# Attention followed by a squared-ReLU FFN on one core: the FFN's second and first matmuls issued in groups of two units

## The chip, the cores and the metric

The kernel runs on 1 core of one Trainium2 chip. The metric is the device time of one launch in microseconds (us), as a median over runs. Before the change it is 187.35 us (three runs: 187.19, 187.35 and 187.91 us).

## What is computed

```python
def phi(x):                                   # S1, S2: 8 x 32
    a = einsum('rd,bhsd->bhsr', S1, x); b = einsum('rd,bhsd->bhsr', S2, x)
    return einsum('bhsi,bhsj->bhsij', a, b).reshape(*x.shape[:-1], 64)
q_p, k_p = phi(q), phi(k)                     # batch 4, heads 4, seq 1088, head_dim 32
kv  = einsum('bhsf,bhsd->bhfd', k_p, v); z = sum(k_p, axis=2)
num = einsum('bhsf,bhfd->bhsd', q_p, kv)
den = einsum('bhsf,bhf->bhs', q_p, z)[..., None] + 1e-06
x   = (num / den) as 4352 tokens x 128
out = square(relu(x @ w_in)) @ w_out          # w_in 128 x 2048, w_out 2048 x 128
```

The inputs and the output are float32. Nearly all arithmetic is in the last line: two matmuls of 4352 x 128 x 2048.

## The kernel before

**Tiling of the FFN.** The 4352 tokens are cut into ten chunks of 256, 384, 448, 448, five of 512, and 256 columns (list FC). The 2048 hidden features are 16 blocks of 128. A *unit* is a piece of one chunk that fills at most one PSUM bank of 512 columns: with 384, 448 or 512 tokens a unit is one hidden block (m = 1), with 256 tokens two blocks (m = 2), except that the first two units of the first chunk have one. There are NU = 145 units: 9, then 16 for each of the eight middle chunks, then 8.

**One unit's work.** mm1 (function ffn1, matmul at L589): the first matmul, w_in block times xT, into a PSUM tile pg. Both operands are float32r; it stands in the trace as one MATMUL for each hidden block. relu (L598): ScalarE (ACT) reads pg from PSUM and writes gt in SBUF. square: gt to g2, on ACT (L606) or VectorE (DVE, L608). mm2 (function ffn2, L627; L622 in the last chunk, with the operands swapped): w_o block times g2, added up over the 16 blocks in a PSUM tile po. Its operands are float32, and it stands in the trace as two MATMULs with a weight load each. When a chunk is done, DVE transposes po (L631) and SyncE stores it (L641).

**Buffers.** pg has 2 PSUM buffers, po 2, gt 4 and g2 6. So mm1 of unit u must wait for relu of unit u-2, and relu of unit u for the square of unit u-4.

**Attention.** For each of the four batches DVE, POOL, ACT and TensorE make the next columns of xT while the FFN of earlier columns runs. On TensorE these are short blocks of small float32 matmuls: kc (L344), kvp (L408), qc (L304) and nd (L542).

**What sets the order.** Each operation is entered in a planner (class `_Order`) with an engine, an estimated duration, a priority and its dependencies; `run` plays the schedule through and emits the instructions in the order of the planned starts. Each engine then executes its own list strictly in that order. For the FFN's matmuls the order is not left to the priorities: a list `seq` is written out by hand (L1055 to L1060), and each matmul is bound to start after the one ahead of it (L1061, L1062). LU = 4 is the lead: mm1 of the first four units comes first, and then mm2 of unit u goes with mm1 of unit u+4, one matmul of each in turn. Where m = 1 that gives mm2(u), mm1(u+4), mm2(u+1), mm1(u+5) and so on. The planner puts attention blocks between these and decides for each square whether ACT or DVE takes it.

Of the kernel before, what the change touches and what calls it, by code (L numbers as in the profile page):

```python
# [104 lines left out]
def kernel(  # L105
# [20 lines left out]
    LU = 4  # L126
# [440 lines left out]
    units, first_unit, dur = [], {}, []  # L567
# [11 lines left out]
    NU = len(units)  # L579
# [21 lines left out]
    def square(u, eng):  # L601
        w = units[u][2] * units[u][4]
        g2 = fpool.tile([128, 512], F32, tag="g2", bufs=G2, name="g2")
        gt = st["gt", u]
        if eng == "ACT":
            nc.scalar.activation(g2[:, 0:w], gt[:, 0:w], Square)  # L606
        else:
            nc.vector.tensor_tensor(out=g2[:, 0:w], in0=gt[:, 0:w], in1=gt[:, 0:w], op=mult)  # L608
        g2s[u] = g2
# [392 lines left out]
    pe1, pe2 = [], []  # L1002
    ends = (NU - 2, NU - 1)
    for u in range(NU):
        ci, c0, n, d0, m = units[u]
        w = n * m
# [7 lines left out]
        for i in range(m):  # L1014
# [14 lines left out]
            lambda eng, u=u: square(u, eng), uses=[("relu", u)], rings=[("g2", G2)],  # L1029
# [23 lines left out]
    hm = len(pe2[-1]) // 2  # L1053
    pe2[-2], pe2[-1] = pe2[-2][:hm] + pe2[-1][:hm], pe2[-2][hm:] + pe2[-1][hm:]
    seq = [x for u in range(LU) for x in pe1[u]]  # L1055
    for u in range(NU):
        p, q_ = list(pe2[u]), list(pe1[u + LU]) if u + LU < NU else []
        while p or q_:
            seq += p[:1] + q_[:1]
            p, q_ = p[1:], q_[1:]  # L1060
    for x, y in zip(seq, seq[1:]):  # L1061
        O.by_name[y]["soft"].append(O.by_name[x])  # L1062
    O.run()
# [30 lines left out]
```

## Time and profile before

| | |
|---|---|
| runs | 187.19, 187.35, 187.91 us; median 187.35 us |
| the profiled execution: span from the first to the last instruction | 186.2 us |
| median of the runs less that span | 1.15 us |
| granted TensorE clock over the span | 1.000 |
| TensorE matmul busy | 180.4 us (97%) |
| ACT busy | 147.1 us (79%) |
| DVE busy | 108.6 us (58%) |
| squares on ACT / on DVE | 122 / 23 |
| relus | 145 |

The page does not give the profiled execution's own device time beside its span; what lies around the span is taken as the difference to the median. Matmuls are pipelined, and their recorded spans overlap, so the starts of matmuls that follow each other say more than the durations. A weight load (PEld) starts when the matmul ahead of its own has begun to stream: the weights that it overwrites are then in use no longer. "idle before" in an instruction's row is the time that its engine had nothing to do, with what ended it.

### The profile page before, as it was taken

To read this page: it belongs to the slowest core of one execution; us is meant where nothing else is said; L and a number is where in the kernel's file an instruction comes from. 1 tells how busy PE (TensorE), PEld (TensorE's weight loads), DVE (VectorE), ACT (ScalarE), POOL (GpSimd) and SP (SyncE) were. 2 spreads that over 40 slices of the span, in tenths; PEclk is the share of its full clock that TensorE was granted. 3 is DMA by queue.
4 is the path that set the end of the run, shared out by engine and by line. 5 is a ranking of instruction groups with operands and counts; after the bars stand their busy time and mean duration, and the time that the engine had idled before them with its cause. 6 is when DMAs were issued, how large, how long until landed. Compare 5 with 4: busy or idle time off the path is not lost.

```text
span 186.2 us, 3768 instructions
## 1 busy us (share of the span) xinstructions
PE 180.4 (97%) x1417; PEld 105.2 (56%) x1418; DVE 108.6 (58%) x242; ACT 147.1 (79%) x281; POOL 36.5 (20%) x162
## 2 busy tenths in 40 slices
PE   8998999999999999999999999999999999999991
PEld 2766766656555566454554545554545554555791
DVE  4979979969982599599324972997122113112210
ACT  3518769868978887797899897897999999988960
POOL 2745405328300000860000003820000000000000
PEclk9999999999999999999999999999999999999999
DMA  5799800100049500001871200002103000300211
GB/s 185 192 297 310 192 4 5 28 4 0 0 55 267 130 2 4 4 0 24 200 186 19 42 0 4 0 0 38 22 0 58 0 0 0 56 0 0 32 28 28
DMA packets 24673, 11.25 MB, mean 60 GB/s; under 512 B 18000, under 2 KB 23120, under 8 KB 24656
## 3 DMA queue, kind: packets, MB, share of 16 engines
q1 hardware_dynamic: 24144, 10.82, 25.0%
q10 hardware_dynamic: 512, 0.20, 0.4%
q8 instruction: 11, 0.18, 0.4%
q14 instruction: 6, 0.05, 0.1%
HBM read 8.78 MB, written 2.23 MB: 59 GB/s over the span
## 4 chain that ended last, share of the span: by engine, by line
PE 90%; DMA 4%; SPq 1%; POOL 1%; issue 1%; DVE 0%; ACT 0%; ACTq 0%
PE po L627 60%; PE pg L589 18%; PE nd L542 3%; DMA w_in<-in_moe_w_in_dram 3%; PE kvp L408 2%; PE pol L622 2%; PE po L622 2%; PE qc L304 2%; DMA s_nat<-in_S_dram 2%; PE kc L344 1%; SPq L194 1%; POOL sfk L789 0%; ACT gt L598 0%; POOL w_in L671 0%; SPq L203 0%
## 5 line engine op out<-in xcount | busy, mean ns | idle before, releaser
L627 PE MATMUL po<-g,w_o 128*128 128x512 f32 (+3 forms) x288 | 133.0, 546 | 0.3 <-PE pg L589 0.3
L589 PE MATMUL pg<-xT,w_in 128*128 128x512 f32 (+3 forms) x160 | 104.8, 665 | 0.6 <-ACT gt L598 0.5
L598 ACT ACTIVATE gt<-pg 128x512 f32<-128x512 f32 (+3 forms) x145 | 80.7, 561 | 21.7 <-PE pg L589 21.2
L606 ACT ACTIVATE g<-gt 128x512 f32<-128x512 f32 (+2 forms) x122 | 71.8, 603 | 2.7
L627 PEld LDWEIGHTS po<-g,w_o 128*128 128x128 f32 x288 | 53.0, 189 | 30.0 <-issue 19.8
L589 PEld LDWEIGHTS pg<-xT,w_in 128*128 128x128 f32 x160 | 30.1, 189 | 31.7 <-issue 14.3
L608 DVE TENSOR_TENSOR g<-gt 128x512 f32<-128x512 f32 (+3 forms) x23 | 15.1, 660 | 45.9 <-ACT gt L598 45.9
L449 POOL COPY kv<-kvt 32x64 f32<-32x64 f32 x48 | 11.7, 243 | 65.4 <-DVE kvt L426 63.3
L503 POOL COPY rd<-rc 32x9 f32<-32x9 f32 (+2 forms) x80 | 16.7, 209 | 13.1 <-DVE rc L495 9.8
L512 DVE STREAM_SHUFFLE qa<-qc 128x576 f32<-128x576 f32 (+2 forms) x20 | 11.6, 652 | 0.0
L527 DVE TENSOR_TENSOR qp<-qa,qb 128x576 f32<-128x576 f32 (+2 forms) x20 | 10.8, 603 | 0.0
L475 DVE STREAM_TRANSPOSE qt<-qc 128x576 f32<-128x576 f32 (+2 forms) x10 | 5.8, 615 | 5.8 <-PE qc L304 5.8
L631 DVE STREAM_TRANSPOSE oT<-po 128x512 f32<-128x512 f32 (+3 forms) x9 | 5.9, 655 | 5.0 <-PE po L627 5.0
L361 DVE TENSOR_TENSOR kp<-fs 128x576 f32<-128x576 f32 x12 | 8.4, 752 | 0.1
L542 PE MATMUL nd<-qp,kv 32*32 32x288 f32 (+2 forms) x320 | 6.8, 353 | 0.0
L559 DVE TENSOR_TENSOR xT<-nd,bc 128x576 fp32r<-128x576 f32 (+2 forms) x10 | 5.6, 600 | 0.9 <-PE nd L542 0.7
L512 DVE STREAM_SHUFFLE qb<-qc 128x576 f32<-128x576 f32 (+2 forms) x10 | 6.0, 648 | 0.0
L542 PEld LDWEIGHTS nd<-qp,kv 32*32 32x32 f32 x320 | 3.8, 103 | 3.8 <-issue 2.2
L297 DVE STREAM_TRANSPOSE qT<-qn 128x192 f32<-128x192 f32 (+3 forms) x11 | 5.9, 566 | 0.0
L552 DVE STREAM_TRANSPOSE bc<-rd 128x576 f32<-128x576 f32 (+2 forms) x10 | 5.8, 602 | 0.2
L622 PE MATMUL pol<-w_o,g 128*128 128x128 f32 x32 | 5.7, 275 | 0.0
L622 PE MATMUL po<-w_o,g 128*128 128x128 f32 x32 | 5.7, 274 | 0.0
(96 smaller groups left out, 92.3 us busy)
## 6 DMA issues: line engine op xcount, KB each, us to landing
kn<-in_k_dram SPq DMA_DIRECT2D x3, 544.0 KB, 5.4
qn<-in_q_dram SPq DMA_DIRECT2D x3, 544.0 KB, 6.9
vn<-in_v_dram SPq DMA_DIRECT2D x9, 144.0 KB, 5.5
w_in<-in_moe_w_in_dram SPq DMA_DIRECT2D x4, 256.0 KB, 5.2
w_o<-in_moe_w_out_dram SPq DMA_DIRECT2D x4, 256.0 KB, 7.1
out_dram<-oT SPq DMA_DIRECT2D x12, 64.0 KB, 2.0
out_dram<-oT SPq DMA_DIRECT2D x8, 56.0 KB, 1.9
out_dram<-oT SPq DMA_DIRECT2D x8, 48.0 KB, 1.8
```

The source lines that it names most:

```text
L361: nc.vector.tensor_tensor(out=_ap(st[b, "kp"], 0, 128, 64 * NT * h, [[64, NT], [8, 8], [1, 8]]), in0=_ap(fs, 0, 128, o, [[32, NT], [1, 8], ...
L449: nc.gpsimd.tensor_copy(_ap(st[b, "kv"], 32 * c, 32, 64 * h, [[32, E], [1, 32]]), _ap(st["kvt"], 32 * h, 32, 0, [[64, E], [1, 32]]),)
L503: nc.gpsimd.tensor_copy(st[b, "rd", i0][32 * h : 32 * h + 32, n * c : n * c + n], st["rc"][32 * c : 32 * c + 32, n * h : n * h + n],)
L512: nc.vector.stream_shuffle(in_=banks(st[b, "qc", i0], 2 * x, 0, m), out=_ap(st[b, which, i0], 0, 128, 2 * m * x, [[m, 2], [1, m]]), mask=m ...
L527: nc.vector.tensor_tensor(out=st[b, "qp", i0, e][:, r], in0=st[b, f"qa{e}", i0][:, r], in1=st[b, "qb", i0][:, r], op=mult,)
L542: nc.tensor.matmul(nd[32 * h : 32 * h + 32, 512 * c : 512 * c + m], kv[r, o : o + 32], qp[r, m * h : m * h + m], start=(e == 0), stop=(e = ...
L589: nc.tensor.matmul(st["pg", u][:, n * i : n * i + n], w_in[:, 128 * (d0 + i) : 128 * (d0 + i) + 128], xT[:, c0 : c0 + n],)
L598: nc.scalar.activation(gt[:, 0:w], st["pg", u][:, 0:w], Relu)
L606: nc.scalar.activation(g2[:, 0:w], gt[:, 0:w], Square)
L608: nc.vector.tensor_tensor(out=g2[:, 0:w], in0=gt[:, 0:w], in1=gt[:, 0:w], op=mult)
L622: nc.tensor.matmul(po[x // 128][:, 0:128], g[:, x : x + 128], w, start=(d == 0), stop=(d == NB - 1),)
L627: nc.tensor.matmul(po[0][:, 0:n], w, g, start=(d == 0), stop=(d == NB - 1))
```

## The change

Only the hand-written list `seq` changes. Instead of one matmul of mm2 and one of mm1 in turn, whole units are listed: for a group of g units, all mm2 of the group and then all mm1 of the group four units on. g is 1 for the units of the first chunk and 2 for all others.

```diff
     seq = [x for u in range(LU) for x in pe1[u]]
-    for u in range(NU):
-        p, q_ = list(pe2[u]), list(pe1[u + LU]) if u + LU < NU else []
-        while p or q_:
-            seq += p[:1] + q_[:1]
-            p, q_ = p[1:], q_[1:]
+    u = 0
+    while u < NU:
+        g = 1 if units[u][0] == 0 else 2
+        seq += [x for w in range(u, u + g) for x in pe2[w]]
+        seq += [x for w in range(u + LU, min(u + LU + g, NU)) for x in pe1[w]]
+        u += g
     for x, y in zip(seq, seq[1:]):
         O.by_name[y]["soft"].append(O.by_name[x])
```

In the middle chunks the order becomes mm2(u), mm2(u+1), mm1(u+4), mm1(u+5), mm2(u+2), mm2(u+3) and so on. In the first chunk, where a unit has two blocks, it becomes mm2, mm2, mm1, mm1 in place of mm2, mm1, mm2, mm1. Number and shape of all matmuls, relus and squares stay the same, and so do all DMAs.

Because the planner plays the new list through, it also places other work differently. In the built program of the changed kernel, 6 pairs of mm1 with 384 columns, 16 with 448 and 40 with 512 stand next to each other, and in the last chunk four groups of four with 256. (The first four mm1 with 384 columns go with units of the first chunk and stay single.) ACT's order becomes relu, relu, square, square, or relu, relu, square where DVE takes the other square; DVE takes 40 squares in place of 23, and ACT 105 in place of 122: of the 66 pairs of units after the four single ones, 29 have both squares on ACT (5 with 384 columns, 11 with 448, 12 with 512, 1 in the last chunk) and 37 have the first unit's square on DVE. The orders of POOL and SyncE are unchanged.

## The prediction

> **What bounds the kernel now.** I first read the busy times and the slices.
>
> ```profile
> PE 180.4 (97%) x1417; PEld 105.2 (56%) x1418; DVE 108.6 (58%) x242; ACT 147.1 (79%) x281; POOL 36.5 (20%) x162
> PE   8998999999999999999999999999999999999991
> ```
>
> TensorE is busy in nine tenths or more of every slice from about 25 us to the last one (one character is 4.65 us), with ACT next at 79%. Busy is not yet bound, so the next view is what TensorE's matmuls waited for, over the whole span:
>
> ```profile
> PE warm L678 <- PEq L1078: 0.8, 1, 0.8
> PE pg L589 <- ACT gt L598: 0.5, 1, 0.5
> PE po L627 <- PE pg L589: 0.3, 1, 0.3
> PE qc L304 <- POOL sfk L789: 0.3, 1, 0.3
> ```
>
> Columns are total, times and longest, in us. The sum is 1.9 us, all of it in the first 21 us. After that no matmul waits for ACT, DVE or a DMA. So a new order of the same matmuls gains only what lies inside a handover from one matmul to the next, or in the first 21 us; it loses wherever it makes a new wait. Next, a steady stretch with 512 columns, from the timeline of all engines (start, duration, instruction):
>
> ```profile
> 130.78 0.58 ACT L598 ACTIVATE gt<-pg 128x512 f32<-128x512 f32 x1
> ...
> 130.90 0.80 PE L589 MATMUL pg<-xT,w_in 128*128 128x512 f32 x1
> 131.30 0.42 PEld L627 LDWEIGHTS po<-g,w_o 128*128 128x128 f32 x2 [0.24 <-issue]
> 131.38 0.63 ACT L606 ACTIVATE g<-gt 128x512 f32<-128x512 f32 x1
> 131.54 1.02 PE L627 MATMUL po<-g,w_o 128*128 128x512 f32 x2
> 131.92 0.58 ACT L598 ACTIVATE gt<-pg 128x512 f32<-128x512 f32 x1
> ...
> 131.99 0.80 PE L589 MATMUL pg<-xT,w_in 128*128 128x512 f32 x1
> ```
>
> A unit takes 131.99 - 130.90 = 1.09 us. In the trace's nanoseconds the two halves of mm2 start 428 apart; mm1 begins to stream where the next weight load starts (131.30), and mm2 follows 234 later (131.54): 428 + 428 + 234 is the unit, nothing left over. ACT alternates: relu to square 0.60, square to the next relu 0.54, 1.14 us for a unit. That is more than TensorE's 1.09, and why one square in four goes to DVE here.
>
> **The change, part by part.** *Same work.* No matmul, activation or DMA is added or removed; SyncE's and POOL's order, so every load and store, stay. What moves: mm1 of the first unit of a pair goes behind one more mm2, 0.86 us later at 512; mm2 of the second goes ahead of it, 0.23 us earlier; ACT runs relu, relu, square, square; 17 squares go to DVE.
>
> *(a) Handovers.* 62 pairs (6, 16 and 40 with 384, 448 and 512 columns) now have mm1 next to mm1. The time from a mm1's begin to the next matmul's start, for a follower that is mm2, is 114 to 117 ns at 256 columns, 170 to 177 at 384, 199 to 205 at 448 and mostly 234 (226 to 236) at 512. A half of mm2 takes 428 for 512 columns streamed twice, 0.417 ns a column and pass, and at that rate the four are 107, 160, 187 and 213. The surplus of mm1 is therefore about 9, 16, 16 and 21 ns. Is it a cost of the change from float32r to float32, which pairs halve, or mm1's own? Only one shape shows both followers before, 256 columns:
>
> ```profile
> 170.26 0.80 PE L589 MATMUL pg<-xT,w_in 128*128 128x256 f32 x2
> 170.66 0.19 PEld L589 LDWEIGHTS pg<-xT,w_in 128*128 128x128 f32 x1 [0.24 <-issue]
> ...
> 170.78 0.30 PEld L627 LDWEIGHTS po<-g,w_o 128*128 128x128 f32 x2
> 170.90 1.02 PE L627 MATMUL po<-g,w_o 128*128 128x512 f32 x2
> ```
>
> The first mm1 begins at 170.66, the second at 170.78, mm2 at 170.90: 119 and 114 ns, and over all such pairs 114 to 119 whichever follows. No saving shows there. A weight load alone delays an idle TensorE by 109, near those 116, so this shape can hide a small one. But the surplus grows with the columns, 9 to 21, as a slower stream would (0.46 ns a column fits all four), and not as a fixed price of a handover. Bounds: 0, and the whole surplus of one mm1 in each pair, 6 x 0.016 + 16 x 0.016 + 40 x 0.021 = 1.2 us. I take 0, the nearer to the 256-column row. Switching to or from an attention block costs 95 ns after mm2 and some 108 after mm1; the 15 blocks change neighbours both ways, at most 15 x 13 ns = 0.2 us of either sign, taken as 0.
>
> The Trainium skill has a rule here (TensorE: Matmul & The Clock Gate, Back-to-back issue gap): columns over 2.4 GHz plus 2.5 ns, so 216 ns for 512. Our 234 is 18 over it, and if the rule held for float32r, those 18 would belong to the handover, 62 pairs would save some 1.1 us, and the time would be 185.9 in place of my 187.0.
>
> *(b) The hole at 19 us.* The timeline of TensorE, its weight loads, and DVE in the first chunk:
>
> ```profile
> 18.65 0.59 PE L627 MATMUL po<-g,w_o 128*128 128x256 f32 x2
> 19.35 0.35 PE L589 MATMUL pg<-xT,w_in 128*128 128x256 f32 x1
> 19.54 0.59 PE L627 MATMUL po<-g,w_o 128*128 128x256 f32 x2
> 20.07 0.96 PE L542 MATMUL nd<-qp,kv 32*32 32x96 f32 x64
> ...
> 19.32 0.19 PEld L589 LDWEIGHTS pg<-xT,w_in 128*128 128x128 f32 x1 [0.48 <-POOL rd L503]
> ...
> 18.40 1.16 DVE L527 TENSOR_TENSOR qp<-qa,qb 128x192 f32<-128x192 f32 x4
> ```
>
> mm2 streams from 18.65 for 2 x 0.215, to 19.08. The mm1 behind it (unit 7) needs the relu of unit 5, which ends at 19.21; its weights load at 19.32 and it enters at 19.43. (The row names POOL; the weight cast that this matmul needs from POOL was done by 15.8, so the relu is the releaser.) That is a hole of 0.35 us. In the new order the second mm2 of unit 3 stands between: 19.08 to 19.51, and by then the relu is done. The nd block behind can start 0.35 earlier, at 19.72, since its last input from DVE is ready at 18.40 + 1.16 = 19.56. From there to the end TensorE waits for nothing, so the 0.35 reaches the end. The holes at 14.6 and 15.5 us lie before the first place where the orders differ. If the gain is lost in nd, it is 0. Term: -0.35 us.
>
> *(c) The relus come in bunches.* For a pair with 512 columns count from the first mm1's entry. The relu starts 0.43 later (entry 132.40, relu 132.83 in the trace, when ACT was free). Independent neighbours on ACT start 0.48 (relu, relu), 0.49 (relu, square), 0.52 (square, square) and 0.54 (square, relu) apart in the closest such places before: 2.03 us for a pair with both squares, against TensorE's 2.18. So the second relu starts at 0.91, the squares at 1.40 and 1.92, done at 2.03 and 2.55; the next pair's relu at 2.61 finds ACT free. mm2 of the first unit enters at 2.65 and its weights can load from 2.42: 0.39 to spare; the second has over 0.8. With 448 columns the spare is 0.27, with 384 only 0.1 (0.17 until it would cost). mm1 of the next pair needs relus that ended by 1.50; it enters at 2.18. Where DVE has the first square, it takes 0.69 from about 1.06, well ahead of 2.42, and ACT needs 0.48 + 0.49 + 0.54 = 1.5 us for a pair. Cost 0; the cover is these spares. The 17 added squares of 0.66 are 11 us of DVE, in stretches where DVE is half idle (after xT of each batch, and after 128 us); the nearest due work behind them, the kT transposes of the next batch, gates a kc block several us later. Cost 0.
>
> The Trainium skill speaks against this part (Perfetto Trace Analysis, Optimizing Tensor Performance): independent matmul groups should rotate through PSUM banks so that the evacuation of one runs beside the next group's matmuls. Two mm1 in a row fill both pg banks before either is read; by that rule a stall could appear, with no figure given, and by the spares above it is 0.
>
> *Sum.* 0 - 0.35 + 0 = -0.35 us on the span of 186.2, so 185.85; with the 1.15 us around it 187.0.
>
> **The rivals.** *Faster: the surplus is the handover's.* 1.2 us more is saved: 187.35 - 0.35 - 1.2 = 185.8. For it: mm2 next to mm2 shows almost no surplus (428 against 426.7), and only mm1 before a float32 matmul was seen above 256 columns. Against it: the growth with columns, and 256.
>
> *Slower: ACT bunching makes mm2 wait.* Place: the 28 pairs of the middle chunks with both squares on ACT. If their pieces ran at today's alternating pace (relu to square plus square to relu: 0.95 at 384, 1.06 at 448, 1.15 at 512), a pair would outlast TensorE's (1.64, 1.91, 2.18) by 0.26, 0.21 and 0.12: 5 x 0.26 + 11 x 0.21 + 12 x 0.12 = 5.1 us, 192.1 as the far end; if the 384 pairs alone do so, 188.3. It decides once ACT is more than 0.17 (384) to 0.4 us (512) late. For it: ACT was already over TensorE's pace. Against it: neighbours in the new order do not need each other's result.
>
> *No gain: the hole stays.* nd or ACT takes back the 0.35: 187.35.
>
> **How the numbers follow.** Chances: forecast 0.38 (187.0, own range 186.7 to 187.3), faster rival 0.36, slower rival 0.20, no gain 0.06. A measurement of this kernel can tell about 0.5%, 0.94 us, from no change; forecast and no gain lie within it, so faster 0.36, same 0.44, slower 0.20. The range goes from 185.7, just under the faster rival's full saving, to 188.3, the slower one with its 384 pairs.
>
> **What would show it.** Right: mm1 to mm1 at 512 columns 226 to 236 ns, a pair every 2.18 us, the weight load of unit 7 without its hole, no new row in TensorE's waits. About 213 to 216 ns between two mm1 would prove the faster rival. Matmuls of L627 waiting for L606 between 28 and 55 us would prove the slower one. Wrong altogether if the granted clock or an attention block's wait differs.

## The result, and the profile after

The changed kernel takes 186.88 us (median of 9 runs, 186.58 to 187.42) beside 187.22 us (9 runs, 187.18 to 187.91) of the kernel before on the same chip: ratio 0.9968, 95% interval 0.9955 to 0.9982. It is some 0.3 us faster, less than the 0.5% from which the prediction counts a change as faster. The time forecast was 187.0 us. Here and below, ratios leave out single runs that came out some 3 us longer, which most kernels showed now and then.

The page of the changed kernel, TensorE's busy time and slices, and the two rows of squares (line, engine, tiles, count | busy us, mean ns | idle before):

```profile
PE 180.0 (97%) x1418; PEld 104.9 (57%) x1418; DVE 120.0 (65%) x259; ACT 135.0 (73%) x264; POOL 36.8 (20%) x162
...
PE   8998999999999999999999999999999999999992
...
L606 ACT ACTIVATE g<-gt 128x512 f32<-128x512 f32 (+2 forms) x105 | 59.9, 602 | 1.4
L608 DVE TENSOR_TENSOR g<-gt 128x512 f32<-128x512 f32 (+3 forms) x40 | 26.6, 666 | 40.6 <-ACT gt L598 40.0
```

The 17 squares moved, 12 us from ACT to DVE, and TensorE's slices look as before. What its matmuls waited for:

```profile
PE warm L678 <- PEq L1079: 0.8, 1, 0.8
PE pg L589 <- ACT gt L598: 0.5, 1, 0.5
```

Two of the four rows of before are left, none is new, and none lies behind 21 us. Now the stretch with 512 columns, to be held against the one in the prediction:

```profile
132.82 1.03 PE L589 MATMUL pg<-xT,w_in 128*128 128x512 f32 x2
133.22 0.19 PEld L589 LDWEIGHTS pg<-xT,w_in 128*128 128x128 f32 x1 [0.24 <-ACT g L606]
133.46 0.42 PEld L627 LDWEIGHTS po<-g,w_o 128*128 128x128 f32 x2
133.65 1.09 ACT L598 ACTIVATE gt<-pg 128x512 f32<-128x512 f32 x2 [0.44 <-PE pg L589]
133.69 1.88 PE L627 MATMUL po<-g,w_o 128*128 128x512 f32 x4
...
134.28 0.69 DVE L608 TENSOR_TENSOR g<-gt 128x512 f32<-128x512 f32 x1 [1.49 <-ACT gt L598]
...
134.77 0.63 ACT L606 ACTIVATE g<-gt 128x512 f32<-128x512 f32 x1
...
135.00 1.03 PE L589 MATMUL pg<-xT,w_in 128*128 128x512 f32 x2
```

A pair takes 135.00 - 132.82 = 2.18 us, twice the 1.09 of a unit before. The weight loads give the handovers: the first mm1 begins at 133.22, the second at 133.46, mm2 enters at 133.69: from a mm1's begin to the next matmul's start, mm1 to mm1 and mm1 to mm2 cost the same within 4 ns (231 and 231 ns at the median of 38 pairs; 201 and 197 at 448 columns, 174 and 172 at 384).

The hole is gone too. TensorE in the first chunk, after:

```profile
17.75 0.74 PEld L627 LDWEIGHTS po<-g,w_o 128*128 128x128 f32 x4
17.87 1.03 PE L627 MATMUL po<-g,w_o 128*128 128x256 f32 x4
18.52 0.19 PEld L589 LDWEIGHTS pg<-xT,w_in 128*128 128x128 f32 x1
...
18.95 0.45 PE L542 MATMUL nd<-qp,kv 32*32 32x96 f32 x32
```

Both mm2 of unit 3 run through (x4, two records each), unit 7's weights load at 18.52 with no idle time in brackets, and nd follows at 18.95. The two profiled spans, though, differ by more than the hole: 186.2 - 184.8 = 1.4 us, where the medians differ by 0.34. Starts of matmuls show the rest. Times are in us, and the first column counts from the start of the span, the next three from the first mm1. The last three columns are the length of the five chunks of 512, from their first mm2 to the first matmul of the last chunk; the time from the start of the last matmul to the end of the span; and the ratio to the kernel before.

| kernel | first mm1 at | first mm2 | first nd | first mm2 of chunk 2 | 512 chunks | behind the last matmul | ratio of times (95%) |
|---|---|---|---|---|---|---|---|
| before (profile shown in the prediction) | 14.04 | 2.10 | 6.03 | 13.86 | 93.96 | 4.00 | |
| before, run again | 13.89 | 1.62 | 5.65 | 13.48 | 93.62 | 4.00 | 0.9995 (0.9986 to 1.0004) |
| alternating, all squares on ACT | 13.60 | 1.59 | 5.65 | 13.48 | 93.62 | 3.81 | 0.9993 (0.998 to 1.0005) |
| groups in the middle chunks alone | 13.89 | 1.59 | 5.65 | 13.48 | 93.87 | 3.81 | 1.0001 (0.9992 to 1.001) |
| changed | 13.54 | 1.63 | 5.41 | 13.24 | 93.95 | 3.81 | 0.9968 (0.9955 to 0.9982) |
| changed, run again | 13.73 | 1.98 | 5.57 | 13.41 | 93.95 | 3.81 | 0.9987 (0.9977 to 0.9997) |
| changed, all squares on ACT | 13.93 | 1.70 | 5.41 | 13.24 | 93.87 | 3.82 | 0.9978 (0.9967 to 0.9989) |
| new order in the first chunk alone | 13.94 | 1.60 | 5.41 | 13.44 | 93.62 | 4.00 | 0.9978 (0.9949 to 1.0007) |
| before, one mm2 moved into the hole | 13.77 | 1.71 | 5.40 | 13.24 | 93.95 | 4.00 | 0.9988 (0.9979 to 0.9998) |
| changed, two relus put ahead | 13.88 | 1.59 | 5.47 | 13.19 | 93.95 | 3.81 | 0.9976 (0.9965 to 0.9987) |
| the same, all squares on ACT | 13.95 | 1.59 | 5.47 | 13.35 | 93.95 | 3.82 | 0.9966 (0.9951 to 0.9981) |

Before against after, the 1.4 us are: a first mm1 0.50 earlier, although TensorE's list is the same up to there; 0.62 up to chunk 2; 0.07 from there to the last matmul; and 0.19 behind it. The 0.62 are the hole (0.24, control against changed kernel: 13.48 and 13.24) and 0.38 that the profile of before had lost to something else (13.86 against 13.48 for the same program), explained below.

Two columns show more than the hole. Behind the last matmul the kernels fall into two groups, 4.00 and 3.81 us: in the longer ones ACT's last drain instruction at the kernel's end begins some 3.65 us after the last matmul's start, in the others some 3.36. The changed kernel is in the shorter group and the kernel before in the longer, so it has 0.19 us less there, in both of its profiles; the kernel with pairs in the middle alone is in the shorter group too. Why the group changes is open, and no run isolates it. Against the control, the 512 chunks of every kernel with groups are 0.25 to 0.33 us longer. The last section comes back to them.

### The profile page after: what moved, and what is told of

Read it like the earlier page. It is cut to its first block, busy times and chain, and to the rows that moved or that the text cites. A ratio compares the mean times of both kernels' runs of the same rounds, so it can differ in the third digit from the quotient of the medians.

```text
span 184.8 us, 3784 instructions
## 1 busy us (share of the span) xinstructions
PE 180.0 (97%) x1418; PEld 104.9 (57%) x1418; DVE 120.0 (65%) x259; ACT 135.0 (73%) x264; POOL 36.8 (20%) x162
## 4 chain that ended last, share of the span: by engine, by line
PE 97%; ACT 0%; DVE 0%; issue 0%
PE po L627 60%; PE pg L589 18%; PE nd L542 4%; PE warm L678 3%; PE kvp L408 2%; PE pol L622 2%; PE po L622 2%; PE qc L304 2%; PE kvp L390 1%; PE kf L314 1%; PE kc L344 1%; PE x L729 1%; ACT gt L598 0%; PE den L794 0%; PE num L794 0%; PE den L754 0%
## 5 line engine op out<-in xcount | busy, mean ns | idle before, releaser
L627 PE MATMUL po<-g,w_o 128*128 128x512 f32 (+3 forms) x288 | 123.5, 547 | 0.0
L598 ACT ACTIVATE gt<-pg 128x512 f32<-128x512 f32 (+3 forms) x145 | 75.1, 568 | 34.6 <-PE pg L589 34.2
L589 PE MATMUL pg<-xT,w_in 128*128 128x512 f32 (+3 forms) x160 | 68.9, 513 | 0.5 <-ACT gt L598 0.5
L606 ACT ACTIVATE g<-gt 128x512 f32<-128x512 f32 (+2 forms) x105 | 59.9, 602 | 1.4
L608 DVE TENSOR_TENSOR g<-gt 128x512 f32<-128x512 f32 (+3 forms) x40 | 26.6, 666 | 40.6 <-ACT gt L598 40.0
L589 PEld LDWEIGHTS pg<-xT,w_in 128*128 128x128 f32 x160 | 28.9, 190 | 29.1 <-ACT gt L598 10.6
L449 POOL COPY kv<-kvt 32x64 f32<-32x64 f32 x48 | 12.3, 256 | 64.8 <-DVE kvt L426 62.7
L678 PE MATMUL warm<-const-bfloat16-1.0 128*128 128x512 bf16 x12 | 5.0, 571 | 0.8 <-PEq L1079 0.8
```

Of the source, the lines that this page charges most:

```text
L449: nc.gpsimd.tensor_copy(_ap(st[b, "kv"], 32 * c, 32, 64 * h, [[32, E], [1, 32]]), _ap(st["kvt"], 32 * h, 32, 0, [[64, E], [1, 32]]),)
L589: nc.tensor.matmul(st["pg", u][:, n * i : n * i + n], w_in[:, 128 * (d0 + i) : 128 * (d0 + i) + 128], xT[:, c0 : c0 + n],)
L598: nc.scalar.activation(gt[:, 0:w], st["pg", u][:, 0:w], Relu)
L627: nc.tensor.matmul(po[0][:, 0:n], w, g, start=(d == 0), stop=(d == NB - 1))
L678: nc.tensor.matmul(t_[:, 0:cols], nc.const_aps.tensor(1.0, (128, 128), mybir.dt.bfloat16), nc.const_aps.tensor(1.0, (128, cols), mybir.dt. ...
```

## The experiments

**Control: the kernel before, unchanged.**

> The kernel before once more, unchanged, for a second profile. Theory (the gain is the hole in the first chunk): ratio 1.000 within 0.002, and the hole of about 0.35 us ahead of unit 7's mm1 is there again. If the first profile was an odd one (its start was slow), the span is nearer 185.4 than 186.2, and the hole may have another size or place.

Ratio 0.9995, span 185.3 us where the first profile had 186.2. Its hole, from the timeline:

```profile
18.08 1.08 ACT L598 ACTIVATE gt<-pg 128x512 f32<-128x512 f32 x2
...
18.22 0.59 PE L627 MATMUL po<-g,w_o 128*128 128x256 f32 x2
18.79 0.19 PEld L589 LDWEIGHTS pg<-xT,w_in 128*128 128x128 f32 x1 [0.38 <-issue]
...
18.90 0.31 PEld L627 LDWEIGHTS po<-g,w_o 128*128 128x128 f32 x2
```

mm2 streams until 18.22 + 0.43 = 18.65; the first of the two relus, which is unit 5's, ends at about 18.7; unit 7's weights load at 18.79 and its mm1 enters at 18.90, where the next weight load starts. The hole is 0.25 us here, not 0.35. Every before-and-after difference inside the span is read against this profile from here on.

**The new order in the first chunk alone, and in the middle chunks alone.**

```diff
     for u in range(NU):
         p, q_ = list(pe2[u]), list(pe1[u + LU]) if u + LU < NU else []
+        if units[u][0] == 0:
+            seq += p + q_
+            continue
         while p or q_:
```

> New order in the first chunk alone (units 0 to 8: whole units in turn), the middle chunks alternate as before. Theory: all of the gain is here, 0.35 us of 187.2, so 186.85, ratio 0.998. Rival (handovers or pairs in the middle): 187.2, ratio 1.000.

```diff
-        g = 1 if units[u][0] == 0 else 2
+        if units[u][0] == 0:
+            p, q_ = list(pe2[u]), list(pe1[u + LU])
+            while p or q_:
+                seq += p[:1] + q_[:1]
+                p, q_ = p[1:], q_[1:]
+            u += 1
+            continue
+        g = 2
```

> Pairs in the middle chunks alone, the first chunk as before. Theory: 187.2, ratio 1.000 (handovers 233 ns whatever follows, spares hold). Rival (the gain is in the middle): 186.9 or less, ratio 0.998 or less. Slower rival (bunched relus): over 187.5.

The first diff is made to the kernel before, the second to the changed one. The middle alone gives 1.0001 (0.9992 to 1.001): no gain from its pairs can be measured. Its profile has two differences from the control that nearly cancel, 0.25 us more in the 512 chunks and 0.19 less behind the last matmul; so 1.0001 bounds their sum, and does not show that each is 0. The first chunk alone gives 0.9978 with an interval that takes in 1. Its nd is 0.24 ahead of the control's like the changed kernel's (5.41 against 5.65), but its chunk 2 comes only 0.04 earlier. DVE's timeline in this run says why:

```profile
22.33 1.37 DVE L285 STREAM_TRANSPOSE kT<-kn 128x576 f32<-128x576 f32 x2 [0.50 <-DMA kn<-in_k_dram]
```

The kc block needs kT, and in this execution the load of k landed only at 22.33, with DVE idle 0.50 in wait for it. The kc block on TensorE lasts 0.84 us, against 0.65 in the changed kernel. In that kernel's profile the same row starts at 21.64 without a wait. The load's time to landing was 8.2 us in the control, 9.0 in the changed kernel and 9.8 here, so the 0.24 gets past the kc block in some executions and can be lost in others.

**Groups of four.**

```diff
-        g = 1 if units[u][0] == 0 else 2
+        g = 1 if units[u][0] == 0 else 4
```

> Groups of four units in the middle chunks in place of two. Two pg buffers: the third and fourth mm1 of a group must wait for the first and second relu. Theory: the third enters at 0.43 + 0.58 + 0.1 + 0.11 = 1.2 us after the first in place of 0.47, the fourth at 1.7 in place of 1.43, so 0.75 + 0.27 = 1.0 us lost in each of 34 groups: about 220 us, with TensorE's weight loads of L590 waiting for L599. Rival (the order does not matter because something else than TensorE's order sets the pace): within 2 us of 187.

217.12 us, a single run (some 220 expected). The wait of TensorE's matmuls, and where it sits:

```profile
PE pg L589 <- ACT gt L598: 12.0, 27, 0.5
```

```profile
135.75 1.03 PE L589 MATMUL pg<-xT,w_in 128*128 128x512 f32 x2
...
136.58 1.09 ACT L598 ACTIVATE gt<-pg 128x512 f32<-128x512 f32 x2 [3.82 <-PE pg L589]
137.23 0.19 PEld L589 LDWEIGHTS pg<-xT,w_in 128*128 128x128 f32 x1 [0.89 <-ACT gt L598]
```

The third mm1 of a group finds both pg banks full and waits until ACT has read the first: from the first mm1's start to the last matmul's end 197.31 us against the control's 167.66, on average 0.87 for each of 34 groups. Over the whole span mm1's weight loads waited 30.3 us for relus, about as much as was lost. This is the stall that the prediction named with the rule on PSUM banks, not the slower rival's, in which mm2 waits for squares; with groups of two it isn't there because the second mm1 needs the bank of two units back, whose relu ended 0.45 us or more before its weights load (units with 512 columns).

**The changed kernel again, and the kernel before with one matmul moved.**

```diff
         p, q_ = list(pe2[u]), list(pe1[u + LU]) if u + LU < NU else []
+        if u == 3:
+            seq += p + q_
+            continue
```

> The changed kernel once more, unchanged, beside new runs of the kernel before: is its 0.3 us real, and what part of its profiled span was a start that happened to be early? If the gain lies in the order, about 0.25 us (0.24 measured at the first nd block, counted from the first mm1), the ratio is again 0.9987 or less, 186.9 to 187.0 beside 187.2. If it was mostly the start (its first mm1 came 0.35 us earlier than in the control), the ratio is 0.999 to 1.0. Every mm1 to mm1 at 512 columns: 228 or 234 ns, as mm1 to mm2 has it.

> The kernel before, with one matmul moved: the second mm2 of unit 3 ahead of the mm1 of unit 7; all else alternates. If the hole at 19 us is where the gain comes from, nd starts 5.41 us after the first mm1 (control 5.65), and as long as k's load for batch 1 has landed by 21.4 us the kc block too comes 0.24 earlier: 186.95, ratio 0.9987. If that load lands later (22.3 in the profile of the run with the first chunk alone, where kc lost all of it), nd gains 0.24 and kc nothing: 187.2, ratio 1.0.

The changed kernel gives 0.9987 this time, the one moved mm2 0.9988 (0.9979 to 0.9998), and nd 5.40 after the first mm1, as expected for a filled hole. One moved mm2 thus makes the gain that the whole change makes beside it. Together with the middle chunks' 1.0001 this shows that the hole is worth its 0.24 us, and that the rest of the change adds nothing that the times can tell. The two intervals of the changed kernel overlap from 0.9977 to 0.9982; what its first comparison shows beyond the hole's 0.24 us is not settled. The 0.19 behind the last matmul is a candidate, which the longer 512 chunks work against.

**All squares on ACT, in the new order and in the old.**

```diff
             {"DVE": dve(w)} if u < ND else
+            {"ACT": 0.095 + w / 1200} if u > 8 else
             {"ACT": 0.095 + w / 1200, "DVE": dve(w)},
```

> The changed kernel with every square of the units after the ninth on ACT, none on DVE: tests the spares of my part (c). By the sum of independent neighbours a pair takes ACT 0.48 + 0.49 + 0.52 + 0.54 = 2.03 us at 512 columns against TensorE's 2.18, so no wait appears: 186.9 to 187.3. By the slower rival (ACT at the alternating pace, 0.26, 0.21 and 0.12 us over per pair at 384, 448 and 512) all 62 pairs lose 6 x 0.26 + 16 x 0.21 + 40 x 0.12 = 9.7 us: 196.6, with rows of L627 waiting for L606.

> The kernel before with every square of the units after the ninth on ACT. If relu and square of one unit follow each other at 0.60 + 0.54 = 1.14 us at 512 (0.95 at 384, 1.06 at 448) and TensorE needs 1.09 (0.82, 0.95), the units lose 0.13 x 12 + 0.11 x 32 + 0.05 x 80 = 9 us: 196. If ACT falls behind until a relu comes ready before the square, its neighbours are independent and it needs only 0.49 + 0.54 = 1.03: 187.2, as with the squares on DVE. The first makes pairs a way to spare DVE, the second makes them worth nothing there too.

No slower rival in either: 0.9978 and 0.9993, and no row in which a matmul waits for a square. The timeline of the pairs with both squares on ACT:

```profile
134.04 1.08 ACT L598 ACTIVATE gt<-pg 128x512 f32<-128x512 f32 x2
134.07 1.88 PE L627 MATMUL po<-g,w_o 128*128 128x512 f32 x4
...
135.01 1.15 ACT L606 ACTIVATE g<-gt 128x512 f32<-128x512 f32 x2
...
136.02 0.42 PEld L627 LDWEIGHTS po<-g,w_o 128*128 128x128 f32 x2
```

The first square takes 0.63, a single one's time, and ends at 135.64; the weights of its mm2 load at 136.02: 0.38 to spare. In the old order the planner, left with ACT alone, bunched ACT's work itself:

```profile
132.37 1.14 ACT L606 ACTIVATE g<-gt 128x512 f32<-128x512 f32 x2
...
133.41 1.24 ACT L598 ACTIVATE gt<-pg 128x512 f32<-128x512 f32 x2
...
134.55 1.14 ACT L606 ACTIVATE g<-gt 128x512 f32<-128x512 f32 x2
```

Two squares, two relus, two squares: 134.55 - 132.37 = 2.18 us for two units, TensorE's pace. The 1.14 us a unit that ACT showed before was the price of relu and square of one unit following each other, not ACT's limit; the slower outcome expected for this run, 196 us, did not come. So DVE's squares, 23 or 40 of them, aren't needed for speed behind the ninth unit.

**Two relus put ahead.** In the changed kernel another hole is left, 0.19 us before unit 5's mm1, which waits for the relu of unit 3 behind the square of unit 2 (the mm2 ahead streams until 15.91 + 0.43 = 16.34, and mm1 enters 0.11 after its weights start to load):

```profile
15.91 0.59 PE L627 MATMUL po<-g,w_o 128*128 128x256 f32 x2
...
16.43 0.30 PEld L589 LDWEIGHTS pg<-xT,w_in 128*128 128x128 f32 x2 [0.32 <-issue]
```

The control has it as well. The edit binds two squares behind the relu of the next unit:

```diff
+    for u in (2, 3):
+        O.by_name[("sq", u)]["soft"].append(O.by_name[("relu", u + 1)])
     O.run()
```

> The changed kernel, with the relus of units 3 and 4 put ahead of the squares of units 2 and 3 on ACT: the hole of 0.19 us that is left, before the mm1 of unit 5 (it waits for the relu of unit 3, which stands behind the square of unit 2), should go. If that hole gates the start, the first mm2 of the second chunk comes 13.05 us after the first mm1 (13.24 in the changed kernel, 13.48 in the control) and the time is 186.75 beside 187.2, ratio 0.9977. If DVE's product for nd, ready 0.18 us ahead of nd now, takes the gain, or the squares come late at mm2 of units 2 and 3, the 13.24 stays: ratio 0.9987.

> The same with every square of the units after the ninth on ACT, which cost nothing in the run of pairs with all squares on ACT: expected as the run before it, 186.7, ratio 0.9975. If fewer squares on DVE in the middle bring something of their own, 0.997 or less; if the relus put ahead bring nothing, 186.9.

0.9976 and 0.9966, both below 1, but not told apart from the changed kernel. The first is close to the 0.9977 expected for a filled hole, but the mark of chunk 2 forbids that reading: it is 13.19, only 0.05 of the 0.19, and not the 13.05 expected. So the agreement is chance. The hole before unit 5 is gone and a smaller one before unit 7 is back (the row of two weight loads; mm2 streams until 18.04 + 0.86 = 18.90, and mm1 enters at about 19.02):

```profile
18.04 1.03 PE L627 MATMUL po<-g,w_o 128*128 128x256 f32 x4
...
18.91 0.30 PEld L589 LDWEIGHTS pg<-xT,w_in 128*128 128x128 f32 x2 [0.25 <-issue]
```

Unit 7 needs the relu of unit 5, and ACT runs two squares ahead of it, from 17.16 to 18.31. Filling one hole moved the shortage of ACT to the next.

## Why the prediction was right, and where it was off

*(a) Handovers: no gain, as forecast.* mm1 to mm1 costs what mm1 to mm2 costs within 4 ns at every width, inside the 226 to 236 forecast at 512 columns, and the middle chunks alone gain nothing. The surplus over the float32 rate is mm1's own, whatever follows it. The faster rival (185.8 us) falls. That the pairs cost nothing is less sure: the 512 chunks took 93.87 or 93.95 us in all six profiles with groups of two, and 93.62 in three of five without. The Trainium skill's 216 ns for 512 columns (TensorE: Matmul & The Clock Gate, Back-to-back issue gap) is not met by this float32r matmul beside either neighbour: 231 was measured. The page gives that figure for an isolated matmul, says that it over-counts in a stream and names no float32r, so the prediction's use of it as the rate of a stream was a misreading; nothing in the sum rested on it.

*(b) The hole: right place, right mechanism, mis-sized.* The term was -0.35 us; with the first mm2 on time it is -0.24 (13.48 in three profiles without the new order in the first chunk, 13.24 in three that fill the hole). It was taken from a profile in which the first mm2 came 0.48 us late. With the first mm2 late like that, 0.34 was saved: between the profile of before and the second profile of the changed kernel nd comes 0.46 earlier, of which the earlier first mm2 is 0.12. Without it, part of the same shortage of ACT shows before unit 5 instead. The sentence that the gain must reach the end because TensorE waits for nothing behind it was too strong: of the seven profiles that fill the hole, chunk 2 has the whole gain in four. A late load of k took most of it back in one, a late xT half of it in another, and in the changed kernel run again the first mm2 came late. So the change of the medians, 0.34 us against 0.35 forecast, agrees better than its term does: the hole gives 0.24 of it, and the rest, where no part is settled, is luck.

*(c) Bunched relus and 17 more squares on DVE: 0, as forecast.* No matmul waits for a square. In pairs with both squares on ACT the usual spares were 0.38 at 512 columns and 0.27 at 448 for the first unit of a pair (0.39 and 0.27 forecast), 0.16 at 384 (0.1 forecast). Least was 0.05, once, in the first pair of the first 448 chunk. The spare of the second unit, "over 0.8", came out as 0.52, harmless: its weights load one half of mm2 behind the first unit's start, at 2.65 + 0.43 = 3.08 in the prediction's count, and its square ends at 2.55. The slower rival falls even with all squares on ACT. The Trainium skill's rule on PSUM banks (Perfetto Trace Analysis, Optimizing Tensor Performance) is kept by two banks and groups of two, and no stall appeared; groups of four, with more units than banks, lost 0.87 us each.

*The sum's base.* The 1.15 us around the span was too little. The changed kernel's profiled execution took 186.58 us for a span of 184.8: 1.78. By that, an estimate, the profiled execution of before took some 188.0, so it was like its slowest run, 187.91, not like the median. The forecast went from the median, so this moved no number but misled on the hole's size. The "no gain" rival (187.35) falls as well: the hole is gone, and of the seven comparisons of kernels that fill it, six have an interval below 1.

## What to carry to other kernels

Where the bottleneck engine never waits in its steady stretch, reordering its own instructions is worth only what a handover costs, and two neighbours that both stand in one trace tell that price before anything is built. A gain then comes from single holes, often at the start; here, moving the one instruction that fills a hole got as much as rewriting the order. Take such a hole's size from more than one execution: loads and helpers that land a few tenths of a microsecond apart change it by half.

## What the runs showed of the hardware

**A DVE square held by a POOL cast.** In the profile of before the first mm2 came 0.48 us later after the first mm1 than in the control, and the row of the waits names an mm1 that was long done. Its weights loaded 0.07 us after the end of DVE's square of unit 0, there and in the changed kernel, so this square is the releaser; and it took twice as long. First the kernel before, then the changed one:

```profile
14.57 1.20 POOL L671 CAST w_in<-w_in 128x512 fp32r<-128x512 f32 x2 [1.00 <-DMA w_in<-in_moe_w_in_dram]
15.22 1.16 DVE L608 TENSOR_TENSOR g<-gt 128x256 f32<-128x256 f32 x2
```

```profile
14.02 0.61 POOL L671 CAST w_in<-w_in 128x512 fp32r<-128x512 f32 x1 [0.70 <-DMA w_in<-in_moe_w_in_dram]
14.66 0.75 DVE L608 TENSOR_TENSOR g<-gt 128x256 f32<-128x256 f32 x2
```

Where the cast runs while the square starts, the two squares take 1.16 us together in place of 0.75: the first one took 0.83, the second 0.41. In four profiles a square met a running cast; each ended 0.27 to 0.28 us after the cast's end. In the control the cast came second, and was the one that was lengthened:

```profile
15.00 0.75 DVE L608 TENSOR_TENSOR g<-gt 128x256 f32<-128x256 f32 x2
...
15.44 0.78 POOL L671 CAST w_in<-w_in 128x512 fp32r<-128x512 f32 x1 [0.48 <-DMA w_in<-in_moe_w_in_dram]
```

That is 0.78 in place of 0.61. In four profiles a cast was lengthened like this; it ended 0.47 us after the square's end each time, whether it had begun 0.16 or 0.36 us before that end. So it waited for the square. The Trainium skill has the rule (SBUF — State Buffer, SBUF: two separate sides): a DVE operation with two inputs in SBUF and a GpSimd operation that reads SBUF share a port pair under an exclusive lock, and whichever comes second waits for all of the first. These rows agree with it. Since the cast starts when a piece of w_in lands, the cost is a matter of the execution. No run moved the cast away, so what that would bring wasn't tried.

**Two levels of the 512-column chunks.** The same program took 93.96 us for these chunks in one profile and 93.62 in another (before, and before run again), all of it in mm1; a unit took 1.093 against 1.087 us at the median; the granted clock over both spans was full, and the float32 matmuls took 428 ns a half in both. The grouped order showed 93.87 and 93.95, never the low level of the alternating one, so the pairs may cost up to some 0.3 us there in place of nothing. What sets the level is open. It is as large as the whole effect of the change, which is why two single profiles would not have told it.
